# Loading v as bf16 through GpSimd's queue, with earlier first weights and the first q ahead of the token ids, in a fused attention and hash-routed expert kernel

## The chip, the cores and the metric

The kernel runs on one core of one Trainium2 chip. The metric is the device time in microseconds (us) of one execution, the median of several runs.

## The reference

Two steps, the second on the output of the first. `q`, `k`, `v` are f32 of shape (8 batches, 8 heads, 576 positions, 64).

```python
q_s = exp(q - max(q, axis=-1));  q_s /= sum(q_s, axis=-1)      # softmax over the 64 features
k_s = exp(k - max(k, axis=2));   k_s /= sum(k_s, axis=2)       # softmax over the 576 positions
kv  = einsum('bhsd,bhse->bhde', k_s, v)                         # 64 x 64 for each head
x   = einsum('bhsd,bhde->bhse', q_s, kv)                        # then (4608 tokens, 512)

expert = token_ids * 2654435761 % 8                             # so: the low three bits decide
for e in range(8):                                              # w1: 512 x 1024, w2: 1024 x 512
    out[expert == e] = relu(x[expert == e] @ w1[e]) @ w2[e]
```

The inputs are small (0.1 times a normal draw), and the kernel leaves the maxima out of both softmaxes.

## The kernel before, in words

**Order of the work.** The kernel keeps one instruction list for each engine (TensorE, VectorE, ScalarE, GpSimd, SP), filled by Python code in program order through `em.op` and `em.dma`. A small tracker (`Buf`, with the tokens of its last writers and readers) puts semaphore waits in front of an instruction where it reads or overwrites what another engine handles. Within an engine everything runs in list order, so the place of a call in the Python text is what sets the order of the work. There is no planner. A load is issued by the engine on whose list it stands: q, k, v and the token ids on SP, the expert weights and the stores on GpSimd. Loads that GpSimd issues may change the type on the way (the weights are f32 in memory and bf16 in SBUF).

**Routing.** The token ids (L288) become expert numbers, one-hot flags `flg` (L331), totals and prefix sums by two matmuls (L338, L339), and from them the position `pos` of each token within its group of 384 or 192 tokens, sorted by expert (L346 to L356). All that is VectorE's work and comes first in its list. `one_hot(b)` (L579) turns positions of batch b into a permutation matrix. `clear()` (L608) has GpSimd write zeros into the sorted activations `xT` once the flags are there. `segment_table()` and `widths()` (L359 to L414), behind batch 0, work out on VectorE and then on GpSimd where each expert's piece of each group goes.

**Stage one: the eight batches.** The loop over b (L734) does, for batch b, with buffers p = b % 2:

- `exp_k(p)` on ScalarE (L504), and `transpose_q(p)`: 18 transposes of exp(q) on TensorE into banks 0 to 2 (L514), copied out by VectorE (L524, L527) and ScalarE (L526);
- `sort(1 - p, ...)` twice: the batch before, times its permutation matrix (L588, 10 matmuls each, banks 3 to 5 and 0 to 2), copied to `xs` by ScalarE (L595); `fill` matmuls (L600) stand before and between, they compute nothing that is used;
- `cast_v(p)`: VectorE copies v from f32 `vf` to bf16 `vx` (L509). `vx` has 65 columns a head, the last of them one, so that the kv matmul sums exp(k) too;
- `load(b + 2, p)`: q, k and v of two batches on, 1,152 KB each, on SP (L495); each waits until its f32 buffer has been read;
- `one_hot(b + 1)` and `exp_q(1 - p, .)` for the next batch;
- `kv(p)`: 36 matmuls of 64 rows into banks 6 and 7, 130 columns each, two heads' v with their ones (L537); the two halves of the array take turns (`h2`). VectorE divides by the sums (L542, L546);
- `qsum(p)` (L556, L560): the sums of exp(q);
- GpSimd's `segments(b - 1)`: 16 copies (L638) of the sorted pieces from `xs` to their places in `xT`, behind 32 register loads (L621);
- `attend(p, ...)`: q times kv (L564), scaled by VectorE into `xn` (L569).

**Stage two: the experts.** For each expert, layer 1 (`l1`, L676, two halves of 320 columns at most) goes through PSUM into `hT` by a relu on ScalarE or VectorE (L683, L685), layer 2 (L701) into `yo` (L711, L713), and GpSimd scatters rows to the output (L717). The first units of layer 1 are mixed with the last batch (L790), and six more follow the last sort (L829), with PSUM banks 6, 3, 0, 6, 3, 0; after these `lslot()` hands out banks 0, 2, 4 in turn.

**Weights.** Four slots in SBUF, each for one w1 and one w2 in bf16, lie over buffers of stage one: slot 0 over qf0 and kf0, slot 1 over vf0 and qf1, slot 2 over kf1 and vf1, slot 3 over the exponentials. The first w1, in two halves (`weights1_half`, L661), is issued by GpSimd in the middle of `segments(5)` and waits for the last k (`R=[b_k[1]]`). The next weights (L653, L667) come in the last batch and after it.

Of the kernel before, what the change touches and what calls it, by code (L numbers as in the profile page):

```python
# [4 lines left out]
F32 = mybir.dt.float32  # L5
BF16 = mybir.dt.bfloat16
# [158 lines left out]
def fused_kernel(nc, q, k, v, moe_token_ids, moe_w1, moe_w2, out):  # L165
# [22 lines left out]
    def at(name, shape, dt, off=None):  # L188
        size = {F32: 4, BF16: 2, F16: 2, I32: 4, I64: 8}[dt]
        for n in shape[1:]:  # L190
            size *= n
        size = (size + 31) // 32 * 32
        if off is None:
            off = cur[0]
            cur[0] += size
        return nc.alloc_sbuf_tensor_at(name, shape, dt, offset=off)

    xT = at("xT", [128, 4, E * CAPS], BF16)
    qkv0 = cur[0]
    qf, kf, vf = [], [], []  # L200
    for i in range(2):
        qf.append(at("qf%d" % i, [128, 4, NC, DH], F32))
        kf.append(at("kf%d" % i, [128, 4, NC, DH], F32))
        vf.append(at("vf%d" % i, [128, 4, NC, DH], F32))
    exp0 = cur[0]
    eq = [at("eq%d" % i, [128, 2, NC, 2, DH], BF16) for i in range(2)]
    ek = [at("ek%d" % i, [128, 2, NC, 2, DH], BF16) for i in range(2)]
    vx0 = cur[0]
    vx = [at("vx%d" % i, [128, 4, NC, DH + 1], BF16) for i in range(2)]
    qT = [at("qT%d" % i, [128, 2, 2, T * 128], BF16) for i in range(2)]  # L210
# [7 lines left out]
    hT = [at("hT%d" % i, [128, FC, CAP], BF16) for i in range(2)]  # L218
    selA = at("selA", [128, B * T, 128], BF16, vx0)
    selB = at("selB", [128, NG * TG, 2, B * T], BF16, vx0 + 10240)  # L220

    w1b, w2b, wreg = [], [], [qkv0, qkv0 + 18432, qkv0 + 36864, exp0]
    for i, o in enumerate(wreg):
# [51 lines left out]
    def gp(fn, R=(), W=(), P=()):  # L275
        em.op("pool", fn, R, W, P)
# [4 lines left out]
    def ac(fn, R=(), W=(), P=()):  # L281
# [4 lines left out]
                             "thr")}  # L286
    b_tok = Buf()
    em.dma("sync", "d_tok", lambda e: e.dma_start(  # L288
        tok64[:], moe_token_ids.rearrange("(b p c) -> p b c", b=B, p=64, c=NC)), P=[b_tok])
    b_vx = [Buf(), Buf()]  # L290
    b_qT = [[Buf() for _ in range(3)] for _ in range(2)]
# [15 lines left out]
    for i in range(2):  # L307
        gp(lambda e, i=i: e.memset(vx[i][:, :, :, DH:DH + 1], 1.0), P=[b_vx[i]])
        gp(lambda e, i=i: e.memset(qT[i][:, :, :, S:T * 128], 1.0), P=b_qT[i])
        for g in range(2):  # L310
            gp(lambda e, i=i, g=g: e.memset(xs[i][:, :, XO[g] + GW[g]:XO[g] + GW[g] + SEG[g]], 0.0), P=b_xs[i])
        for h in range(2):
            dv(lambda e, i=i, h=h: e.memset(kvn[i][64 * h:64 * h + 64, :, 1 - h, :], 0.0), P=[b_kvn[i]])
# [169 lines left out]

    b_q, b_k, b_v = [Buf(), Buf()], [Buf(), Buf()], [Buf(), Buf()]
    b_eq = [[Buf(), Buf()] for _ in range(2)]
# [7 lines left out]
    def load(b, p):  # L493
        for nm, dst, src, bb in (("d_q%d", qf, q, b_q), ("d_k%d", kf, k, b_k), ("d_v%d", vf, v, b_v)):
            em.dma("sync", nm % p, lambda e, dst=dst, src=src: e.dma_start(  # L495
                dst[p][:].rearrange("p h c d -> p h (c d)"),
                src[b].rearrange("(a h) (p c) d -> (h p) a (c d)", h=2, p=64)), W=[bb[p]])

# [4 lines left out]
    def exp_k(p):  # L503
        ac(lambda e: e.activation(ek[p][:].rearrange("p j c a d -> p a (j c) d"),  # L504
                                  kf[p][:].rearrange("p (a j) c d -> p a (j c) d", a=2), ACTF.Exp),
           R=[b_k[p]], W=[b_ek[p]])

    def cast_v(p):
        dv(lambda e: e.tensor_copy(out=vx[p][:, :, :, 0:DH], in_=vf[p][:]), R=[b_v[p]], W=[b_vx[p]])  # L509

# [19 lines left out]

    def kv(p):
        fns = []
        for j in range(2):
            for c in range(NC):
                for h2 in range(2):
                    r = slice(64 * h2, 64 * h2 + 64)
                    fns.append(lambda e, j=j, c=c, h2=h2, r=r: e.matmul(  # L537
                        PB[:, 6 + h2, 130 * j:130 * j + 130], ek[p][r, j, c, :, :].rearrange("p a d -> p (a d)"),
                        vx[p][r, j::2, c, :], start=(c == 0), stop=(c == NC - 1)))
        em.op("pe", fns, R=[b_ek[p], b_vx[p]], W=[bk[6], bk[7]])  # L540
        KV = PB[:, 6:8, 0:260].rearrange("p h (j a x) -> p j h a x", j=2, a=2)
        dv(lambda e: e.reciprocal(out=rk[p][:].rearrange("p (j h) -> p j h", h=2), in_=KV[:, :, :, 0, 64]),  # L542
           R=[bk[6], bk[7]], W=[b_rk[p]])
        for a in range(2):
            r = slice(64 * a, 64 * a + 64)
            dv(lambda e, a=a, r=r: e.tensor_tensor(  # L546
                out=kvn[p][r, :, a, :].rearrange("p (j h) x -> p j h x", h=2), in0=KV[r, :, :, a, 0:DH],
                in1=rk[p][r, :].rearrange("p (j h) -> p j h", h=2).unsqueeze(3).to_broadcast([64, 2, 2, DH]),
                op=ALU.mult), R=[bk[6], bk[7], b_rk[p]], W=([b_kvn[p]] if a == 0 else ()),
               P=(() if a == 0 else [b_kvn[p]]))  # L550
# [176 lines left out]

    load(0, 0)
    load(1, 1)
    clear()  # L730
    one_hot(0)
    exp_q(0, 0)
    exp_q(0, 1)
    for b in range(B):  # L734
# [4 lines left out]
        if b > 0:  # L739
# [5 lines left out]
            sort(1 - p, 2, 0)  # L745
        cast_v(p)
        if b + 2 < B:
            load(b + 2, p)
        if not last:
            one_hot(b + 1)  # L750
            exp_q(1 - p, 0)
            exp_q(1 - p, 1)
        kv(p)
        qsum(p)
        if b == B - 2:
            for s, bs in enumerate(([b_q[0], b_k[0]], [b_v[0], b_q[1]])):
                b_w1[s], b_w2[s] = [Buf(*bs), Buf(*bs)], Buf(*bs)
            load_segments(b - 1, "pool")
            sg = segments(b - 1)
            run(sg, 8)  # L760
            weights1_half(0, 0, 0, R=[b_k[1]])
            weights1_half(0, 0, 1)
            run(sg)
        elif last:
            weights1(1, 1)
            weights2(0, 0)
            for x in (b - 1, b):
                load_segments(x, "pool", 1)
                load_segments(x, "dve", 0)
            run(segments(b - 1, "pool", 1))  # L770
        elif b > 0:
            load_segments(b - 1, "pool")
            run(segments(b - 1))
# [12 lines left out]

    for s, bs in ((2, [b_k[1], b_v[1]]), (3, b_eq[0] + b_eq[1] + b_ek)):
        b_w1[s], b_w2[s] = [Buf(*bs), Buf(*bs)], Buf(*bs)
# [40 lines left out]
    for i, (ee, f) in enumerate([(0, f) for f in range(FC // 2, FC, 2)] + [(1, f) for f in range(0, FC, 2)]):  # L829
        l1(ee, f, 0, (6, 3, 0)[i % 3], True)  # L830
    for f in range(0, FC, 2):
# [38 lines left out]
    fresh = lambda: Buf(every)  # L870
    for lst in (b_q, b_k, b_v, b_ek, b_vx, b_kvn, b_rk, b_rq, bk):
        lst[:] = [fresh() for _ in lst]
# [24 lines left out]
    b_xg, b_id, b_yg = [fresh() for _ in range(4)], fresh(), [fresh() for _ in range(T)]  # L897
    dv(lambda e: e.memset(vx[0][:, :, :, DH:DH + 1], 1.0), P=[b_vx[0]], R=[every])
    dv(lambda e: e.memset(qT[0][:, :, :, S:T * 128], 1.0), P=b_qT[0])
# [6 lines left out]
    for b in range(B):  # L906
        load(b, 0)
        exp_q(0, 0)
        exp_q(0, 1)
        exp_k(0)  # L910
        cast_v(0)
        transpose_q(0)
        kv(0)
        qsum(0)
# [67 lines left out]
```

## Time and profile before

| | us |
|---|---|
| median of 3 runs | 228.6 (228.36 to 228.71) |
| the profiled execution, its time | 228.91 |
| its span, first to last instruction | 227.1 |
| TensorE busy, matmuls | 199.1 (88% of the span) |
| TensorE, weight loads | 130.9 (58%) |
| VectorE | 123.8 (55%) |
| GpSimd | 118.0 (52%) |
| ScalarE | 106.6 (47%) |

The core read 61.90 MB and wrote 10.49 MB of HBM. The median time from issue to landing was 15.3 us for q, 15.6 for k, 15.4 for v (eight each), 2.4 us for the token ids (36 KB), and 5.6 us for each of the four pieces of the first w1.

The profile names lines of the kernel (L537 is line 537) and engines: PE is TensorE, PEld its weight loads, DVE VectorE, ACT ScalarE, POOL GpSimd, SP the engine that issues plain loads. A timeline line gives the start, the busy time, the engine, the line, the operation, what is written <- what is read, the number of instructions, and in brackets how long the engine had stood idle and who released it. The forty digits are tenths of busy time in slices of 5.7 us. In the GB/s row a casting load counts by the bytes written.

### The profile page before, as it was taken

How to read it: one execution, taken by the hardware profiler on the slowest of the kernel's cores; microseconds unless marked ns; L12 is line 12 of the kernel's file. 1: busy time of each engine (PE TensorE's matmuls, PEld its weight loads, DVE VectorE, ACT ScalarE, POOL GpSimd, SP SyncE). 2: the span in 40 equal slices, each digit the busy share in tenths (PEclk: the TensorE clock that was granted, in tenths of full speed). 3: DMA queues.
4: the chain of work that ended last, by engine and by line, in shares of the span. 5: the costliest groups of instructions: out<-in, count | busy, mean ns of one | idle time of the engine just before them, and what ended most of it. 6: DMA issues, size and time to landing. Idle time of an engine off the chain costs nothing.

```text
span 227.1 us, 4693 instructions
## 1 busy us (share of the span) xinstructions
PE 199.1 (88%) x1804; PEld 130.9 (58%) x1828; DVE 123.8 (55%) x273; ACT 106.6 (47%) x133; POOL 118.0 (52%) x227
## 2 busy tenths in 40 slices
PE   0538868999989789899999999999999999999990
PEld 0336546767667566674664854754845845846640
DVE  5778999888988845999912412411422412412220
ACT  3548687797888826654541331332322322422311
POOL 6500859894584993940007975706616525035053
PEclk9999999999999999999999999999999999999996
DMA  5999999999999999999964899999999798113032
GB/s 144 403 391 393 390 389 391 391 392 389 389 390 389 243 170 195 160 184 205 211 113 185 155 193 205 365 244 209 273 203 279 123 208 238 42 46 149 16 123 101
DMA packets 29775, 54.96 MB, mean 242 GB/s; under 512 B 2351, under 2 KB 11567, under 8 KB 29744
## 3 DMA queue, kind: packets, MB, share of 16 engines
q0 software_dynamic: 16544, 26.22, 55.0%
q1 hardware_dynamic: 13200, 28.35, 33.9%
q8 instruction: 16, 0.26, 0.5%
q14 instruction: 15, 0.12, 0.2%
HBM read 61.90 MB, written 10.49 MB: 319 GB/s over the span
## 4 chain that ended last, share of the span: by engine, by line
PE 63%; DVE 12%; DMA 12%; issue 4%; POOL 3%; ACT 2%; SPq 2%; POOLq 1%; DVEq 0%; ACTq 0%
PE ps L701 29%; PE ps L676 24%; DMA kf<-in_k_dram 7%; DMA vf<-in_v_dram 5%; DVE xn L569 4%; PE ps L588 4%; PE ps L537 2%; SPq L495 2%; POOL xT L638 2%; PE ps L564 1%; DVE vx L509 1%; DVE kvn L546 1%; ACT eq L500 1%; PE ps L600 1%; DVE zz L436 1%
## 5 line engine op out<-in xcount | busy, mean ns | idle before, releaser
L717 POOL DMA_INDIRECT out_dram<-yo,idx x40 | 39.5, 988 | 72.6 <-ACT yo L711 31.9
L701 PE MATMUL ps<-w2b,hT 128*128 128x512 bf16 x312 | 68.6, 379 | 0.4
L676 PE MATMUL ps<-xT,w1b 128*128 128x320 bf16 (+1 forms) x512 | 64.6, 286 | 1.7 <-DVE cs L438 0.9
L676 PEld LDWEIGHTS ps<-xT,w1b 128*128 128x128 bf16 x512 | 49.7, 98 | 16.1 <-DVE cs L438 1.2
L701 PEld LDWEIGHTS ps<-w2b,hT 128*128 128x128 bf16 x320 | 31.2, 98 | 36.3
L638 POOL COPY xT<-xs x112 | 42.1, 433 | 16.6 <-ACT xs L595 14.2
L683 ACT ACTIVATE hT<-ps 128x640 bf16<-128x640 f32 x41 | 28.8, 703 | 40.0 <-PE ps L676 39.6
L711 ACT ACTIVATE yo<-ps 128x512 f32<-128x512 f32 x26 | 15.5, 597 | 54.1 <-PE ps L701 54.1
L685 DVE TENSOR_SCALAR hT<-ps 128x640 bf16<-128x640 f32 x23 | 19.0, 824 | 30.2 <-PE ps L676 30.2
L713 DVE COPY yo<-ps 128x512 f32<-128x512 f32 x14 | 9.7, 691 | 44.0 <-PE ps L701 44.0
L588 PE MATMUL ps<-oneh,xn 128*128 128x384 bf16 (+1 forms) x160 | 23.4, 295 | 3.3 <-DVE xn L569 2.8
L569 DVE TENSOR_TENSOR xn<-ps,rq 128x1024 bf16<-128x1024 f32 (+1 forms) x24 | 23.6, 1039 | 4.2 <-PE ps L564 4.2
L588 PEld LDWEIGHTS ps<-oneh,xn 128*128 128x128 bf16 x160 | 14.4, 97 | 14.4 <-DVE xn L569 5.7
L595 ACT ACTIVATE xs<-ps 128x768 bf16<-128x768 f32 (+1 forms) x32 | 19.0, 647 | 7.0 <-PE ps L588 6.8
L500 ACT ACTIVATE eq<-qf 128x1152 bf16<-128x1152 f32 x16 | 17.7, 1159 | 8.5 <-DMA qf<-in_q_dram 8.5
L504 ACT ACTIVATE ek<-kf 128x2304 bf16<-128x2304 f32 x8 | 17.0, 2124 | 4.9 <-DMA kf<-in_k_dram 4.8
L537 PE MATMUL ps<-vx,ek 64*128 64x130 bf16 x288 | 10.6, 228 | 4.0 <-DVE vx L509 4.0
L514 PE MATMUL ps<-ident,eq 128*128 128x128 bf16 x144 | 10.5, 231 | 2.8 <-ACT eq L500 1.9
L667 POOL DMA_DIRECT2D w2b<-in_moe_w_dram x16 | 12.4, 803 | 0.0
L537 PEld LDWEIGHTS ps<-vx,ek 64*128 64x128 bf16 x288 | 9.2, 99 | 5.4 <-issue 5.2
L564 PEld LDWEIGHTS ps<-kvn,qT 128*128 128x128 bf16 x160 | 9.3, 99 | 5.2 <-DVE kvn L546 5.1
L600 PE MATMUL ps<-ones,ident 128*128 128x512 bf16 x26 | 9.2, 390 | 3.3 <-DVE qT L527 2.3
(102 smaller groups left out, 146.8 us busy)
## 6 DMA issues: line engine op xcount, KB each, us to landing
qf<-in_q_dram SPq DMA_DIRECT2D x8, 1152.0 KB, 15.3
kf<-in_k_dram SPq DMA_DIRECT2D x8, 1152.0 KB, 15.6
vf<-in_v_dram SPq DMA_DIRECT2D x8, 1152.0 KB, 15.4
w2b<-in_moe_w_dram POOLq DMA_DIRECT2D x16, 512.0 KB, 12.2
w1b<-in_moe_w_dram POOLq DMA_DIRECT2D x14, 512.0 KB, 10.3
w1b<-in_moe_w_dram POOLq DMA_DIRECT2D x4, 256.0 KB, 5.6
out_dram<-yo,idx POOLq DMA_INDIRECT x40, 4.1
tok<-in_moe_token_ids_dram SPq DMA_DIRECT2D x1, 36.0 KB, 2.4
```

What stands on the lines that cost most here:

```text
L500: ac(lambda e: e.activation(eq[p][:, j, :, :, :].rearrange("p c a d -> p a c d"), qf[p][:, j::2, :, :], ACTF.Exp), R=[b_q[p]], W=[b_eq[p][j]])
L504: ac(lambda e: e.activation(ek[p][:].rearrange("p j c a d -> p a (j c) d"), kf[p][:].rearrange("p (a j) c d -> p a (j c) d", a=2), ACTF.Ex ...
L537: fns.append(lambda e, j=j, c=c, h2=h2, r=r: e.matmul(PB[:, 6 + h2, 130 * j:130 * j + 130], ek[p][r, j, c, :, :].rearrange("p a d -> p (a ...
L569: dv(lambda e: e.tensor_tensor(out=xn[p][:, t0:t0 + n, :].rearrange("p t (g x) -> p (t g) x", x=DH), in0=PB[:, bank:bank + n, :].rearrange ...
L588: em.op("pe", [lambda e, g=g, i=i, k=k, n=n: e.matmul(PB[:, bank + (k if g == 0 else 2), (0 if g == 0 else GW[1] * k):(GW[0] if g == 0 els ...
L595: ac(lambda e, g=g, src=src: e.activation(xs[p][:, c0:c0 + 2, XO[g]:XO[g] + GW[g]], src, ACTF.Copy), R=bs, P=b_xs[p][c0:c0 + 2])
L638: return e.tensor_copy(out=xT[:, :, bass.ds(do, SEG[g])], in_=xs[p][:, :, XO[g]:XO[g] + GW[g] + SEG[g]][:, :, bass.ds(so, SEG[g])])
L676: em.op("pe", [lambda e, d=d, k=k: e.matmul(cut(PB[:, u + k, 0:H2]), w1b[s][:, d, 128 * (f + k):128 * (f + k) + 128], cut(rhs(d)), start=( ...
L683: ac(lambda e: e.activation(o, i, ACTF.Relu), R=bk[u:u + 2], W=[b_hT[hp][hf][f // 2]])
L685: dv(lambda e: e.tensor_scalar(out=o, in0=i, scalar1=0.0, scalar2=None, op0=ALU.max), R=bk[u:u + 2], W=[b_hT[hp][hf][f // 2]])
L701: em.op("pe", [lambda e, fc=fc: e.matmul(PB[:, u, :], hT[hp][:, fc, 128 * t:128 * t + 128], w2b[s][:, fc, :], start=(fc == 0), stop=(fc == ...
L717: em.dma("pool", "d_o%d" % y, lambda e: e.indirect_dma_start(out=out[:, :], out_offset=IndirectOffsetOnAxis(ap=idx[:, 5 * ee + t:5 * ee + ...
```

## The change

- v is no longer loaded as f32 by SP and cast by VectorE. A new `load_v` on GpSimd's list loads it straight into bf16, into one of four buffers: `vx` is now two tensors, each `[128, 5, 2, 9, 64]`, with a block of ones in the middle (index 2) and one v on either side of it (indices 0, 1 and 3, 4).
- v of batch b + 1 is issued in batch b, ahead of `segments(b - 1)` on GpSimd; the first two right at the start, ahead of `clear()`, the first of them waiting for the first q.
- `kv` reads three blocks of 64 columns (two heads and the ones), so its matmuls have 192 columns in place of 130.
- The first q is issued ahead of the token ids on SP. `one_hot(0)` moves from ahead of the loop to behind the first transposes.
- Without vf, slot 1 lies over qf1 and kf1, slot 2 over the exponentials, slot 3 over vx. The first w1 is issued right behind the last v and ahead of all of `segments(5)`; it no longer waits for the last k.
- The six units of layer 1 use banks 6, 3, 0, 6, 4, 2.

The same lines change in the branch for overflowing experts, which this input does not enter. The diff without that branch:

```diff
-    vx = [at("vx%d" % i, [128, 4, NC, DH + 1], BF16) for i in range(2)]
+    vx = [at("vx%d" % i, [128, 5, 2, NC, DH], BF16) for i in range(2)]
...
-    w1b, w2b, wreg = [], [], [qkv0, qkv0 + 18432, qkv0 + 36864, exp0]
+    w1b, w2b, wreg = [], [], [qkv0, qkv0 + 18432, exp0, vx0]
...
+    def load_one(nm, dst, src, b, p, bb):
+        em.dma("sync", nm % p, lambda e: e.dma_start(
+            dst[p][:].rearrange("p h c d -> p h (c d)"),
+            src[b].rearrange("(a h) (p c) d -> (h p) a (c d)", h=2, p=64)), W=[bb[p]])
+
+    load_one("d_q%d", qf, q, 0, 0, b_q)
     em.dma("sync", "d_tok", lambda e: e.dma_start(
         tok64[:], moe_token_ids.rearrange("(b p c) -> p b c", b=B, p=64, c=NC)), P=[b_tok])
-    b_vx = [Buf(), Buf()]
+    b_vx = [Buf() for _ in range(4)]
...
-        gp(lambda e, i=i: e.memset(vx[i][:, :, :, DH:DH + 1], 1.0), P=[b_vx[i]])
+        gp(lambda e, i=i: e.memset(vx[i][:, 2, :, :, :], 1.0), P=b_vx[2 * i:2 * i + 2])
...
+        load_one("d_q%d", qf, q, b, p, b_q)
+        load_one("d_k%d", kf, k, b, p, b_k)
+
+    def load_v(b, n, R=()):
+        o = 3 * (n % 2)
+        em.dma("pool", "d_v%d" % n, lambda e: e.dma_start(
+            vx[n // 2][:, o:o + 2, :, :, :].rearrange("p a j c d -> p (a j) (c d)"),
+            v[b].rearrange("(a h) (p c) d -> (h p) a (c d)", h=2, p=64)), R=R, W=[b_vx[n]])
...
-    def cast_v(p):
-        dv(lambda e: e.tensor_copy(out=vx[p][:, :, :, 0:DH], in_=vf[p][:]), R=[b_v[p]], W=[b_vx[p]])
...
-    def kv(p):
+    def kv(p, n):
+        o, one = (0, 2) if n % 2 == 0 else (2, 0)
+        a0 = 1 - one // 2
...
-                        PB[:, 6 + h2, 130 * j:130 * j + 130], ek[p][r, j, c, :, :].rearrange("p a d -> p (a d)"),
-                        vx[p][r, j::2, c, :], start=(c == 0), stop=(c == NC - 1)))
+                        PB[:, 6 + h2, 192 * j:192 * j + 192], ek[p][r, j, c, :, :].rearrange("p a d -> p (a d)"),
+                        vx[n // 2][r, o:o + 3, j, c, :], start=(c == 0), stop=(c == NC - 1)))
...
-    load(0, 0)
+    load_one("d_k%d", kf, k, 0, 0, b_k)
     load(1, 1)
+    load_v(0, 0, R=[b_q[0]])
+    load_v(1, 1)
     clear()
-    one_hot(0)
     exp_q(0, 0)
     exp_q(0, 1)
...
-        cast_v(p)
+        if b == 0:
+            one_hot(0)
...
-        kv(p)
+        kv(p, b % 4)
         qsum(p)
+        if 0 < b < B - 1:
+            load_v(b + 1, (b + 1) % 4)
         if b == B - 2:
-            for s, bs in enumerate(([b_q[0], b_k[0]], [b_v[0], b_q[1]])):
+            for s, bs in enumerate(([b_q[0], b_k[0]], [b_q[1], b_k[1]])):
                 b_w1[s], b_w2[s] = [Buf(*bs), Buf(*bs)], Buf(*bs)
+            weights1_half(0, 0, 0)
+            weights1_half(0, 0, 1)
             load_segments(b - 1, "pool")
-            sg = segments(b - 1)
-            run(sg, 8)
-            weights1_half(0, 0, 0, R=[b_k[1]])
-            weights1_half(0, 0, 1)
-            run(sg)
+            run(segments(b - 1))
...
-    for s, bs in ((2, [b_k[1], b_v[1]]), (3, b_eq[0] + b_eq[1] + b_ek)):
+    for s, bs in ((2, b_eq[0] + b_eq[1] + b_ek), (3, b_vx)):
...
-        l1(ee, f, 0, (6, 3, 0)[i % 3], True)
+        l1(ee, f, 0, (6, 3, 0, 6, 4, 2)[i], True)
```

## The prediction

> **What bounds the kernel now.** I read the page's forty slices first, then the chain of waits, then the timelines of TensorE, VectorE and GpSimd one by one.
>
> ```profile
> PE   0538868999989789899999999999999999999990
> DMA  5999999999999999999964899999999798113032
> GB/s 144 403 391 393 390 389 391 391 392 389 389 390 389 243 170 195 160 184 205 211 113 185 155 193 205 365 244 209 273 203 279 123 208 238 42 46 149 16 123 101
> ```
>
> The loads run at 390 GB/s up to about 75 us, so stage one (attention and routing of the eight batches) looks bound by them. From 97 us TensorE is full to the end (99.5% busy in each stretch of 10 us from 100 to 220) and nothing there waits for a weight. So the end moves with the time at which stage one hands over. What paces stage one has to be read from one turn of its loop:
>
> ```profile
> 58.78 1.48 PE L588 MATMUL ps<-oneh,xn 128*128 128x384 bf16 x10 [0.34 <-DVE xn L569]
> 60.32 0.38 PE L600 MATMUL ps<-ones,ident 128*128 128x512 bf16 x1
> 60.54 1.47 PE L588 MATMUL ps<-oneh,xn 128*128 128x384 bf16 x10
> 61.94 1.21 PE L537 MATMUL ps<-vx,ek 64*128 64x130 bf16 x36
> 63.08 0.65 PE L556 MATMUL ps<-pair,qT 128*128 128x2 bf16 x20
> 64.34 1.29 PE L564 MATMUL ps<-kvn,qT 128*128 128x128 bf16 x20 [0.15 <-DVE kvn L546]
> 67.41 1.48 PE L588 MATMUL ps<-oneh,xn 128*128 128x384 bf16 x10 [0.34 <-DVE xn L569]
> ```
>
> ```profile
> 60.04 1.35 DVE L509 CAST vx<-vf 128x2304 bf16<-128x2304 f32 x1
> 61.71 1.14 DVE L579 TENSOR_SCALAR oneh<-col,pos 128x384 bf16<-128x384 f16 x5 [0.32 <-PE ps L588]
> 63.19 0.18 DVE L542 RECIPROCAL rk<-ps 128x4 f32<-128x4 f32 x1 [0.34 <-PE ps L537]
> 63.41 0.87 DVE L546 TENSOR_TENSOR kvn<-ps,rk 64x256 bf16<-64x256 f32 x2
> 65.00 2.95 DVE L569 TENSOR_TENSOR xn<-ps,rq 128x1024 bf16<-128x1024 f32 x3 [0.28 <-PE ps L564]
> ```
>
> A loop that bites its tail: sort (L588), fill, sort, kv (L537), then VectorE's kvn, attend (L564), two pieces of xn, and sort again. 58.78 to 67.41 is 8.63 us. The kv groups start at 25.51, 35.53, 44.69, 53.31, 61.94, 70.56 and 79.47, so three turns of 8.62. The loads need 9.0 us a batch (landings of k at 56.90, 65.88, 74.89); they had a lead and catch up only at the last k (kv at 79.47, 0.29 late). The cast at 60.04 ends at 61.39, and VectorE then waits for TensorE twice: it lies beside the loop. kv lies on it.
>
> ```profile
> 28.86 0.19 POOL L414 CAST widei<-wide 128x8 int32<-128x8 f32 x1
> 31.33 13.43 POOL L638 COPY xT<-xs  x32 [2.28 <-issue]
> 45.91 5.50 POOL L638 COPY xT<-xs  x16 [1.15 <-ACT xs L595]
> 54.53 5.49 POOL L638 COPY xT<-xs  x16 [3.12 <-ACT xs L595]
> ```
>
> GpSimd has a backlog from 23 to 45 us (routing tables until 29.05, 2.3 us of register loads, 32 segment copies), then room.
>
> **What the Trainium skill says.** "DMA: Bandwidth & Descriptors", section "SWDGE vs HWDGE vs iDMA": a casting load must come from GpSimd, and each DMA engine takes turns between GpSimd's and SP's queues. So a v load beside q and k loads gets about half the rate; no trace line of before shows the two kinds contending for long (casting w1 meets the last v only at 75 to 78 us), so this is unproven here. "SBUF — State Buffer", section "Who interferes with whom": VectorE's two-port operations block GpSimd. The trace fits (L638 copies took 0.42 us each at 31 to 45 us, 0.34 later), and a v load's descriptors could suffer so too. "TensorE: Matmul & The Clock Gate", section "Wait — 56ns, not 53.3ns?": time goes by columns, at half speed when cold. It agrees: 8 matmuls of 320 columns in L676 start 1.09 us apart per group, 0.426 ns a column; the first kv, after idle time, took 2.13 us against 1.21.
>
> **The change, part by part.**
>
> *Cast removed, 8 x 1.36 us of VectorE.* Covered in turns 3 to 6, as shown. In turns 1 and 2 sort ends as late as the cast (kv at 25.51, the cast ends 25.26), so no gain there. In the last turn the cast ran 77.78 to 79.14 and the second sort ended at 79.5: a tie. Gain 0; bounds 0 to -0.3.
>
> *kv wider.* The ones become a third block of 64 columns: 192 instead of 2 x 65 = 130. Two halves of the array run as a pair. Now 36 matmuls take 1.15 us start to start of the next group (61.94 to 63.08), 64 ns a pair. 192 columns at 0.426 ns are 82 ns: 18 x 82 = 1.47 us, +0.33 a batch. All of it is on the loop, for kv(1) to kv(7): 7 x 0.33 = **+2.3**. Bounds: 2.2, as 82 does not fit into 64, to 3.8, if the 1.15 scales by 192/130. A gain is excluded.
>
> *Start.* q0 issues at 0.80 instead of 1.60 and lands near 5.9 instead of 7.3. The token ids now queue behind q0: landing near 6.8 instead of 3.2. VectorE needed 7.8 us from them to the positions (3.27 to 11.01), so positions at 13.5 to 14.6. In VectorE's order the q transposes' copies (0.96) and one_hot(0) and (1) (2.27) follow: free at 16.8 to 17.8. The old order had VectorE take up 1/kv sums at 17.04. v0 waits on GpSimd for q0, is issued near 6.2 and shares with k0 and q1: data from 7.3 to 13.3, landing 14.4, close to the old cast's end (14.72). But the cold kv(0) grows from 2.13 to about 3.0 us: 17.4. So the sums come 0.4 to 0.8 later. k1, after six loads rather than five, lands near 22 instead of 19.39; its exp (2.12) and the ScalarE copy (1.00) end at 25.1, then the second sort 1.4, kv(1) near 26.5. Between these I take **+0.8** at kv(1); bounds 0 to 1.5. The memsets of the ones grow from 36 to 1152 columns; the nearest row (960 f32 columns, 0.85 us) says under 1.6 us in all: GpSimd is free at 6.1 instead of 4.5, covered by the wait for q0. clear() waits for flags later, with GpSimd idle until 23 anyway.
>
> *v loads queued on GpSimd.* Each issue costs about 0.8 us there (L667, as many rows: 0.803). v2 stands behind the routing tables, whose end was 29.05 and moves to about 29.7. A casting load of about that size takes from 7.6 us (L667's least for 1.05 MB of source) to 9 at half rate (an estimate, from the first page's turn-taking), with q4 and k4 queued on SP: v2 lands at 36 to 39, say 37.9. kv(2) would be ready at 26.3 + 10.02 + 0.33 = 36.65. **+1.3** for the wait; bounds 0 to 2.5. Behind it on GpSimd the copies start later: 2.3 + 16 copies = 8 us, v3 issued near 39.5, landing 47.5, just when kv(3) is ready (37.9 + 9.16 + 0.33 = 47.4). After that a turn of GpSimd is 0.8 + 2.3 + 5.5 = 8.6 us against a turn of the loop of 8.95, and v is issued 11 us ahead: covered. If copies stay at 0.42 us the turn is 9.8 and the cover is gone, 0.85 a turn.
>
> *q and k alone on SP* run ahead, so the last k is no longer waited for: **-0.3**.
>
> *Weights.* w1(0) is issued behind v7, before the segment copies of batch 5, instead of between them. By then k7 has landed, by the above, so no one waits; were it not so, 2.1 MB of source, 5.3 us of loading, would share with k7, up to 2.6 us. First use of w1b was at 82.94, without a wait, so no gain either. Copies start 2.7 us later, GpSimd having had 3.1 us idle there. Region 1 now waits for exp of k7 (done by about 81), region 3 for kv(7): both before GpSimd gets to them. Cost 0, bounds -0.2 to +0.5.
>
> *Banks 6,3,0,6,4,2.* TensorE stood from 95.90 to 96.77; VectorE's cs is named, but that matmul needs bank 0, which ScalarE emptied at 96.62. The new order frees it: **-0.9**; 0 if something else was late.
>
> Sum: 2.3 + 0.8 + 1.3 - 0.3 - 0.9 = +3.2 us. The profiled execution took 228.91 (span 227.1 and 1.8 around it): 232.1. It lies 0.3 above the median, so 231.8 against 228.6.
>
> **Rivals.** *Faster, 226.9:* the loads or VectorE pace the loop after all. For it: 390 GB/s without a gap, VectorE 86 to 95% busy. Then 0.8 us of earlier loads brings k7 to 74.1 and kv(7), 4.6 us behind it, to 78.7; the wider kv hides in TensorE's waits, and with the banks 228.9 - 0.8 - 0.9 = 227.2, median 226.9. Against it: turns of 8.62, shorter than the loads' 9.0. It decides if kv costs under 0.1 us a turn and v2 is in time. *v late every turn, 235:* copies at 0.42 us or descriptors blocked, 4 turns x 0.85 = 3.4 on top: 235.2. Against: 0.34 us copies from 45 us on. *No difference, 228.6:* v2 in time, no loss at the start, kv at half its price.
>
> **How the numbers follow.** Forecast 0.60, its own range 229.6 (all low ends) to 234.5 (all high ends together would be 236); faster rival 0.20; late v 0.12; no difference 0.08. A measurement of this kernel tells 0.2% from no change. The range 227.0 to 235.0 leaves out half of the faster rival, half of the late v and a little of the forecast. Faster 0.20, same 0.08, slower 0.72.
>
> **What would show it.** kv groups of 64x192 taking 1.5 us and turns near 8.95; kv(2) waiting for DMA of v at about 38; kv(1) near 26.3; kv(7) near 83; no stop of TensorE ahead of L676's last third. I am wrong if kv groups still take 1.2 us, or kv(7) starts before 80.

## The result, and the profile after

The changed kernel takes 233.93 us (median of four runs, 233.78 to 234.02) against 228.66 for the kernel before on the same chip: the ratio is 1.0229, with a 95% interval of 1.0211 to 1.0247. It is slower, as forecast, but by 5.3 us where the forecast said 3.2. The profiled execution took 234.02, its span 232.3 (before: 228.91 and 227.1).

The page of the kernel after: the slices of TensorE and of the loads, the kv group, and how long a v load takes from issue to landing.

```profile
PE   0408796899998987999999999999999999999990
...
DMA  6999999999997999769993699999999799213023
GB/s 210 367 292 305 397 290 314 311 377 301 297 370 161 144 185 202 120 84 199 205 212 105 172 189 206 269 327 203 292 196 244 169 187 241 83 45 140 21 104 117
...
L547 PE MATMUL ps<-vx,ek 64*128 64x192 bf16 x288 | 14.7, 258 | 6.5 <-DMA vx<-in_v_dram 6.5
...
vx<-in_v_dram POOLq DMA_DIRECT2D x8, 576.0 KB, 9.6
```

Three things are to be seen. The GB/s row is below before's even 390 in most slices up to 69 us: a casting load counts by the bytes written, half of those read, so that 290 to 315 means both kinds at once and not idle DMA engines (the DMA row stays at 9 there). The kv group has 64x192 where it had 64x130. And its one large wait in the whole run, 6.5 us, is for a DMA of v. In which turn that is, the chain of waits tells at its head:

```profile
0.79 6.06 DMA qf<-in_q_dram
7.16 10.95 DMA vx<-in_v_dram
18.20 3.08 PE ps L547 x36
```

The very first kv waits: v0 is issued at 7.16, soon after q0 has landed, and lands 10.95 us later. TensorE's timeline of the kernel before has this group 3.33 us earlier, behind the cast:

```profile
14.87 2.13 PE L537 MATMUL ps<-vx,ek 64*128 64x130 bf16 x36 [4.01 <-DVE vx L509]
```

Here is a turn of the loop later on, TensorE's timeline of the kernel after (kv is L547 now, sort L598, attend L574):

```profile
64.52 1.48 PE L598 MATMUL ps<-oneh,xn 128*128 128x384 bf16 x10 [0.34 <-DVE xn L579]
66.06 0.38 PE L610 MATMUL ps<-ones,ident 128*128 128x512 bf16 x1
66.28 1.47 PE L598 MATMUL ps<-oneh,xn 128*128 128x384 bf16 x10
67.67 1.66 PE L547 MATMUL ps<-vx,ek 64*128 64x192 bf16 x36
69.27 0.65 PE L566 MATMUL ps<-pair,qT 128*128 128x2 bf16 x20
70.52 1.29 PE L574 MATMUL ps<-kvn,qT 128*128 128x128 bf16 x20 [0.15 <-DVE kvn L556]
73.59 1.48 PE L598 MATMUL ps<-oneh,xn 128*128 128x384 bf16 x10 [0.34 <-DVE xn L579]
```

It is the old turn with the same two small waits and nothing new but a longer kv: 64.52 to 73.59 is 9.07 us instead of 8.63, and from the start of kv to the next group 1.60 instead of 1.14.

The starts of the kv groups say where the time came from (us):

| | kv(0) | kv(1) | kv(2) | kv(3) | kv(6) | kv(7) | span |
|---|---|---|---|---|---|---|---|
| before | 14.87 | 25.51 | 35.53 | 44.69 | 70.56 | 79.47 | 227.1 |
| after | 18.20 | 29.47 | 39.95 | 49.53 | 76.75 | 85.38 | 232.3 |
| difference | 3.33 | 3.96 | 4.42 | 4.84 | 6.19 | 5.91 | 5.2 |

Of the 5.2 us, 3.96 are there at kv(1). From kv(1) to kv(6) five turns add 2.23, 0.45 each, the width of kv; the last turn gives back 0.28 although its kv is wider too. Behind kv(7) come a last 0.45 of kv, -1.04 where the banks changed (below), and -0.1 that I can't assign.

### The profile page after: what moved, and what is told of

Its sections match the earlier page's. It is cut to its first block, busy times and chain, and to the rows that moved or that the text cites. A ratio compares the mean times of both kernels' runs of the same rounds, so it can differ in the third digit from the quotient of the medians.

```text
span 232.3 us, 4687 instructions
## 1 busy us (share of the span) xinstructions
PE 202.2 (87%) x1804; PEld 134.6 (58%) x1828; DVE 112.8 (49%) x265; ACT 106.7 (46%) x133; POOL 121.1 (52%) x235
## 4 chain that ended last, share of the span: by engine, by line
PE 74%; DVE 13%; DMA 7%; issue 3%; DVEq 1%; POOL 1%; POOLq 0%
PE ps L711 29%; PE ps L686 26%; PE ps L598 8%; DVE xn L579 7%; PE ps L547 6%; DMA vx<-in_v_dram 5%; DVE kvn L556 3%; DMA qf<-in_q_dram 3%; PE ps L574 2%; PE ps L610 1%; DVEq L634 1%; POOL out_dram L727 1%; DVE rk L552 1%; PE ps L823 1%; DVE qT L532 1%
## 5 line engine op out<-in xcount | busy, mean ns | idle before, releaser
L686 PE MATMUL ps<-xT,w1b 128*128 128x320 bf16 (+1 forms) x512 | 64.4, 286 | 0.8 <-ACT hT L693 0.8
L686 PEld LDWEIGHTS ps<-xT,w1b 128*128 128x128 bf16 x512 | 49.8, 98 | 14.9 <-ACT hT L693 1.1
L648 POOL COPY xT<-xs x112 | 39.1, 407 | 19.4 <-ACT xs L605 17.9
L598 PE MATMUL ps<-oneh,xn 128*128 128x384 bf16 (+1 forms) x160 | 23.2, 294 | 2.8 <-DVE xn L579 2.8
L598 PEld LDWEIGHTS ps<-oneh,xn 128*128 128x128 bf16 x160 | 14.5, 98 | 13.6 <-DVE xn L579 5.7
L547 PE MATMUL ps<-vx,ek 64*128 64x192 bf16 x288 | 14.7, 258 | 6.5 <-DMA vx<-in_v_dram 6.5
L547 PEld LDWEIGHTS ps<-vx,ek 64*128 64x128 bf16 x288 | 12.8, 100 | 7.8 <-issue 7.7
L589 DVE TENSOR_SCALAR oneh<-col,pos 128x384 bf16<-128x384 f16 (+1 forms) x40 | 9.9, 317 | 9.8 <-PE ps L598 9.8
L574 PEld LDWEIGHTS ps<-kvn,qT 128*128 128x128 bf16 x160 | 9.0, 98 | 5.1 <-DVE kvn L556 5.1
```

The source lines that it names most:

```text
L547: fns.append(lambda e, j=j, c=c, h2=h2, r=r: e.matmul(PB[:, 6 + h2, 192 * j:192 * j + 192], ek[p][r, j, c, :, :].rearrange("p a d -> p (a ...
L598: em.op("pe", [lambda e, g=g, i=i, k=k, n=n: e.matmul(PB[:, bank + (k if g == 0 else 2), (0 if g == 0 else GW[1] * k):(GW[0] if g == 0 els ...
L648: return e.tensor_copy(out=xT[:, :, bass.ds(do, SEG[g])], in_=xs[p][:, :, XO[g]:XO[g] + GW[g] + SEG[g]][:, :, bass.ds(so, SEG[g])])
L686: em.op("pe", [lambda e, d=d, k=k: e.matmul(cut(PB[:, u + k, 0:H2]), w1b[s][:, d, 128 * (f + k):128 * (f + k) + 128], cut(rhs(d)), start=( ...
```

## The experiments

All times are medians; ratios are to the kernel before on the same chip, with a 95% interval. Line numbers shift by a few lines between the kernels. The theories after the result: *the loop of TensorE and VectorE paces stage one from kv(1) on, and the order in which the loads' bytes come paces it before that.* The rivals: the token ids, now behind q0, hold the start (VectorE's routing chain); v loads come late in every turn; the loads pace the loop, so kv's width counts for little.

### kv with 128 columns

```diff
-        o, one = (0, 2) if n % 2 == 0 else (2, 0)
-        a0 = 1 - one // 2
+        o = 3 * (n % 2)
...
-                        PB[:, 6 + h2, 192 * j:192 * j + 192], ek[p][r, j, c, :, :].rearrange("p a d -> p (a d)"),
-                        vx[n // 2][r, o:o + 3, j, c, :], start=(c == 0), stop=(c == NC - 1)))
+                        PB[:, 6 + h2, 128 * j:128 * j + 128], ek[p][r, j, c, :, :].rearrange("p a d -> p (a d)"),
+                        vx[n // 2][r, o:o + 2, j, c, :], start=(c == 0), stop=(c == NC - 1)))
```

> The changed kernel with 128 columns in each kv matmul: the block of ones is not read, so the sums of exp(k) are left out and the division uses a column of v instead. If the wider kv lies on the loop (theory), kv groups take about 1.15 us again, the turn falls from 9.07 to 8.62 us, the cold first kv from 3.06 to 2.1, and the time by 7 x 0.45 + 0.95 = 4.1 us, to about 229.8. If the loads or another engine pace the loop (rival), the turn stays near 9.0 and the time falls by less than 1.3 us.

Measured: 230.93, ratio 1.0094 (1.0063 to 1.0126), so 3.1 us of the 5.3 gone. TensorE's timeline of this kernel:

```profile
39.70 1.18 PE L546 MATMUL ps<-vx,ek 64*128 64x128 bf16 x36 [0.55 <-DMA vx<-in_v_dram]
48.79 1.18 PE L546 MATMUL ps<-vx,ek 64*128 64x128 bf16 x36
57.38 1.18 PE L546 MATMUL ps<-vx,ek 64*128 64x128 bf16 x36
65.97 1.18 PE L546 MATMUL ps<-vx,ek 64*128 64x128 bf16 x36
```

The turns are 8.59 again (57.38 to 65.97): the whole step from 8.6 to 9.07 is kv's columns, and a loop paced by loads would not have moved. The gain is 1.0 us less than expected. About half of that is lost by kv(1): the cold first kv takes 0.95 us less (2.11), but attend behind it takes 2.34 us instead of 1.29, and kv(1) comes only 0.47 earlier, at 29.00. The first of the lines above has the other half: kv(2) could start a little earlier than in the kernel after, and now waits 0.55 us for v2. The kernel after reaches kv(2) at 39.95, where a weight load waits 0.2 us for v2 and no matmul does: the load is the next ceiling, just above.

### Cast taken out of the kernel before

Two runs. In the first, nothing is cast and v is left out of the result:

```diff
-        cast_v(p)
...
-        gp(lambda e, i=i: e.memset(vx[i][:, :, :, DH:DH + 1], 1.0), P=[b_vx[i]])
+        gp(lambda e, i=i: e.memset(vx[i][:], 1.0), P=[b_vx[i]])
```

> The kernel before without VectorE's cast of v: v is loaded as before, but kv reads constants, so v is left out of the result. If the cast lay beside the loop (prediction), turns 3 to 6 stay at 8.62 us and only the start gains, where the first kv no longer waits for v0 and its cast (14.87 before, about 13.6 then): the time falls by 0.5 to 1.5 us, to about 227.6. If VectorE paced the loop (rival), each turn falls by up to 1.36 us until the loads stop it at 9.0 a batch or TensorE does, and the time falls by 2 us or more.

Measured: 229.0, ratio 1.001 (0.9998 to 1.0022). The turns are as before (kv at 63.08 and 71.70), but the memsets of the whole `vx`, 2.04 us each on GpSimd, disturbed the start of this kernel (last section), so its total decides nothing. In the second, the first two batches are cast as ever and the others not:

```diff
-        cast_v(p)
+        if b < 2:
+            cast_v(p)
```

> The kernel before with VectorE's cast of v for batches 0 and 1 only; the later batches use the v of these (the products with v are wrong from batch 2 on), so that the start is undisturbed. If the cast lies beside the loop (theory), turns 3 to 6 stay at 8.62 us and the time falls by 0 to 0.3 us. If VectorE paces the loop (rival), the time falls by 1 us or more, as far as the loads, 9.0 us a batch, let it.

Measured: 228.81, ratio 0.9994 (0.9985 to 1.0004). VectorE's timeline, and then TensorE's, of this kernel:

```profile
62.07 1.14 DVE L579 TENSOR_SCALAR oneh<-col,pos 128x384 bf16<-128x384 f16 x5 [1.59 <-PE ps L588]
```

```profile
62.29 1.21 PE L537 MATMUL ps<-vx,ek 64*128 64x130 bf16 x36
70.92 1.21 PE L537 MATMUL ps<-vx,ek 64*128 64x130 bf16 x36
```

Where VectorE did the cast it now stands idle for 1.59 us and waits for TensorE's sort; the turn is 8.63. The cast lay beside the loop, and taking eight of them from VectorE (its busy time fell from 123.8 to 112.8 us in the kernel after) bought nothing.

### v0 ahead of everything on GpSimd

```diff
+    em.dma("pool", "d_v0", lambda e: e.dma_start(
+        vx[0][:, 0:2, :, :, :].rearrange("p a j c d -> p (a j) (c d)"),
+        v[0].rearrange("(a h) (p c) d -> (h p) a (c d)", h=2, p=64)), W=[b_vx[0]])
     b_qT = [[Buf() for _ in range(3)] for _ in range(2)]
...
-    load_v(0, 0, R=[b_q[0]])
```

> The changed kernel with v of batch 0 issued as the first entry of GpSimd's list, without waiting for the first q. If v0 was late because its bytes stood behind those of q1 and k1 (theory), kv(0) starts near 14.5 instead of 18.20 and the time falls by 3.0 to 3.7 us, to about 230.6. If the token ids behind q0 set the start (rival: VectorE is busy with them and with the permutations until 17.06), the division still starts near 20 or later, and the time falls by at most 1.3 us. A third case: q0 and k0 are delayed by v0 by as much as is won, and the time is unchanged.

Measured: 234.33, ratio 1.0238 (1.0206 to 1.0271): a miss, no gain at all. TensorE's timeline, then GpSimd's:

```profile
14.55 3.06 PE L550 MATMUL ps<-vx,ek 64*128 64x192 bf16 x36 [1.50 <-DVE prod L362]
...
26.90 1.66 PE L550 MATMUL ps<-vx,ek 64*128 64x192 bf16 x36
...
40.01 2.94 PE L550 MATMUL ps<-vx,ek 64*128 64x192 bf16 x36 [2.54 <-DMA vx<-in_v_dram]
```

```profile
29.26 0.88 POOL L509 DMA_DIRECT2D vx<-in_v_dram  x1
```

kv(0) starts at 14.55 with the token ids still behind q0, and the division at 18.33, not near 20. In the kernel after, then, the ids do not hold the start: VectorE is through with them at 17.06 and stands idle for 4.25 us before the division. They are next in line, though. Here v0 also shares with the ids, VectorE gets them at 8.84 instead of 7.21, and it goes from its last permutation to the division without a pause. kv(1) comes 2.6 us earlier than in the kernel after, and there the gain ends: kv(2) waits 2.54 us for v2, which GpSimd issues at 29.26 and whose bytes appear only after 32 us (the rate falls from 394 to 275 GB/s from 32 on), when k3 is nearly in; and after the pause kv(2) itself takes 2.94 us instead of 1.66. So the late v0 had hidden the wait for v2 that I had predicted.

### q1 and k1 held back until k0 has landed

```diff
+    em.raw("sync", lambda e: None, R=[b_k[0]])
     load(1, 1)
     load_v(0, 0, R=[b_q[0]])
```

> The changed kernel with SP waiting for the landing of k0 before it issues q1 and k1; v0 is still issued at about 7.2 us. If v0 was late because of bytes queued ahead of it (theory), its bytes now follow k0 at once, it lands near 12.5 and the DMA rate has no gap between 9 and 11 us; kv(0) then starts 4 to 5 us earlier, but q1 and k1 come 2 to 4 us later, and the time falls by 1 to 3 us. If a casting load from GpSimd takes 3.7 us from its issue to its first byte whatever is in the queue (rival), the DMA rate falls to near zero between about 9 and 11 us and v0 lands near 15.

Measured: 234.37, ratio 1.0241 (1.0206 to 1.0275). The total is a miss, but the start answers the question of why v0 is late. Here are stretches of one microsecond of the kernel after (start and end, length, busy time and number of instructions of TensorE, its weight loads, VectorE, ScalarE and GpSimd; the last three columns are the granted clock, the DMA engines' busy share and GB/s):

```profile
10.00:11.00 1.00, 1.00 (x13) 1.00 (x11) 0.97 (x2) 0.98 (x1) 1.00 (x2) 1.00 1.07 396
11.00:12.00 1.00, 0.71 (x7) 0.44 (x5) 0.94 (x2) 1.00 (x1) 1.00 (x2) 1.00 1.08 349
12.00:13.00 1.00, 0.00 (x0) 0.00 (x0) 0.96 (x2) 1.00 (x2) 0.38 (x1) 1.00 1.12 282
13.00:14.00 1.00, 0.00 (x0) 0.00 (x0) 0.86 (x3) 0.27 (x2) 0.00 (x0) 1.00 1.14 293
```

And of this kernel, with q1 and k1 held back:

```profile
8.00:9.00 1.00, 0.07 (x1) 0.07 (x2) 0.81 (x3) 1.00 (x2) 0.95 (x3) 1.00 1.04 374
9.00:10.00 1.00, 1.00 (x7) 0.66 (x8) 0.21 (x1) 0.15 (x2) 1.00 (x2) 1.00 0.96 108
10.00:11.00 1.00, 1.00 (x12) 1.00 (x11) 0.97 (x2) 1.00 (x1) 1.00 (x2) 1.00 1.09 182
11.00:12.00 1.00, 0.67 (x7) 0.41 (x4) 0.93 (x3) 1.00 (x2) 1.00 (x2) 1.00 1.20 192
```

In the kernel after, the rate stays at 390 to 396 GB/s until 11 us, which is what plain loads do alone; only then does it fall to 282 to 296, where a casting load shares with a plain one. v0 was issued at 7.16, so its bytes began more than four microseconds later. SP had issued q0, k0, q1 and k1 by 4.1 us. Here SP holds q1 and k1 back until 9.89. v0 is issued at the same time, 7.12, and the rate drops to 108 to 192 GB/s as soon as k0 is in: the bytes are v0's own, and kv(0) starts at 13.75. That refutes the rival of 3.7 us from the issue whatever is queued.

The packets in the traces carry the queue they came from, and they set a limit to the theory. In the kernel after, the first packet of v0 moves at 11.55 us, behind the rest of k0 and four fifths of q1; the last of q1 and all of k1, issued before it, share with it. In this run it moves at 8.95, with the last packets of k0. In all runs that load v in this way, wherever a v was issued behind the first 7 us with GpSimd's queue empty, the first packet came 1.4 to 1.8 us later if SP had at most 0.6 of a load issued and not yet moved, 3.0 to 3.2 us later if it had 1.1 to 1.2 loads, and 3.8 to 4.4 us later, never more, if it had 1.4 to 2.7. So in these runs such a load waits for what SP has issued, but for one and a half loads of 1,152 KB at the most.

kv(1) still comes 2.29 us earlier than in the kernel after, at 27.18. All of it is lost on the way to kv(2), at 40.50: a stall of VectorE at 34 us takes 1.4 us and a slow sort behind it 1.3 (both in the last section). Without them little would have been left either, since v2's last packet moves at 39.09.

### Every v a batch earlier

v0 first as above, and v of batch b + 2 issued in batch b:

```diff
-        if 0 < b < B - 1:
-            load_v(b + 1, (b + 1) % 4)
+        if b < B - 2:
+            load_v(b + 2, (b + 2) % 4)
```

> The changed kernel with v0 as GpSimd's first entry, as in the run that issued it first, and every later v issued one batch earlier, so that v2 stands ahead of the routing tables on GpSimd. Theory now: two ceilings lie side by side at kv(2). The late v0 holds it at 39.95 us, and v2, landing near 39.8, holds it at 40 when v0 is early; so only both together gain. Then kv(1) starts near 26.9, kv(2) near 37.4, no matmul waits for a load of v, and the time falls by 2.5 us against the changed kernel, to about 231.4. Rival: the early loads of v hold up q1 and k1, kv(1) comes 2 us later than 26.9 and the time falls by less than 1 us.

Measured: 235.68, ratio 1.0309 (1.0282 to 1.0335), the worst of all: the rival of this run came true. ScalarE's timeline, then TensorE's:

```profile
25.24 2.12 ACT L518 ACTIVATE ek<-kf 128x2304 bf16<-128x2304 f32 x1 [4.58 <-DMA kf<-in_k_dram]
```

```profile
28.33 2.74 PE L601 MATMUL ps<-oneh,xn 128*128 128x384 bf16 x10 [3.14 <-ACT qT L537]
31.01 1.75 PE L550 MATMUL ps<-vx,ek 64*128 64x192 bf16 x36
```

v2, issued at 13.63, took its share of the rate while k1 was still coming: v2's packets move from 17.9 to 25.1 us, and k1's last at 23.3, against 20.5 with v0 alone moved ahead. exp of k1 begins at 25.24 (19.86 in the kernel after), ScalarE's copy of qT stands behind it, the sort behind that, and kv(1) starts at 31.01.

The same with kv of 128 columns, to see whether the width still counts in full when v is early:

```diff
+                        PB[:, 6 + h2, 128 * j:128 * j + 128], ek[p][r, j, c, :, :].rearrange("p a d -> p (a d)"),
+                        vx[n // 2][r, o:o + 2, j, c, :], start=(c == 0), stop=(c == NC - 1)))
...
+        if b < B - 2:
+            load_v(b + 2, (b + 2) % 4)
```

> The same with 128 columns in each kv matmul (the sums of exp(k) left out, the division by a column of v). If the change's loss consists of the start, the wait for v2 and the wider kv (theory), nothing of it is left but the gain of the banks: turns of 8.62 us, kv(7) near 79.8, and 227.3 us, 1.4 below the kernel before. If something else of the change costs time (rival), it stays above 228.7.

Measured: 231.95, ratio 1.0132 (1.0114 to 1.015). Against the run before it, on the same chip, that is 3.7 us (3.6 between the two profiled spans). From kv(2) to kv(7) it takes 43.04 us against 45.45: 2.41 less in five turns, so the width counts in full here too. Ahead of that it was 1.85 us ahead at kv(1) and lost 1.09 of it by kv(2), where VectorE stalled (last section). By the sign set for this run, the total above 228.7, something else costs time, and that is the order of the loads: I had taken early v as free, and kv(1) comes at 29.16.

### v2 behind k1

The kernel with every v a batch earlier, with kv of 192 columns and one wait more: v2 is issued when k1 has landed.

```diff
-            load_v(b + 2, (b + 2) % 4)
+            load_v(b + 2, (b + 2) % 4, R=[b_k[1]] if b == 0 else ())
```

> As the run that issued every v one batch earlier, but with the load of v2 waiting on GpSimd for the landing of k1. Theory now: until kv(2) the loads are the bound and only their order counts; v0 early held kv(2) by v2, v2 early held kv(1) by k1. With v2 right behind k1 the bytes come in the order in which they are needed: kv(1) starts near 26.9, kv(2) near 37.4, and the time is 2.5 us below the changed kernel, about 231.4; what is left against the kernel before is the wider kv. Rival: GpSimd's loads cost the start in any order (their descriptors, their ports, or the ids behind q0); then kv(2) starts at 39 or later again and the time stays above 233.4.

Measured: 231.43, ratio 1.0111 (1.0094 to 1.0128), as expected. GpSimd's timeline, then TensorE's:

```profile
21.76 0.74 POOL L509 DMA_DIRECT2D vx<-in_v_dram  x1 [8.22 <-DMA kf<-in_k_dram]
```

```profile
26.71 1.66 PE L550 MATMUL ps<-vx,ek 64*128 64x192 bf16 x36
...
37.59 1.66 PE L550 MATMUL ps<-vx,ek 64*128 64x192 bf16 x36
```

No matmul waits for v any more. kv(1) is 1.20 us later than before, kv(2) 2.06, and from there on each turn adds 0.45. With the bytes in the order of need, 2.5 us of the change's loss are gone, without a change of any amount of work: 233.93 to 231.43. That order is v0, then q1 and k1, then q2 and k2, with v2 joining in at 25.83 us, when three quarters of k2 are in. What is left against the kernel before: 1.20 at the start, about what the ids behind q0 cost alone (next run); 0.41 more in the turn to kv(2), of which 0.34 is one subtraction of VectorE that takes 0.50 us instead of 0.16 (last section); 3.15 of width; less 0.73, 1.04 and 0.1 for the last turn, the banks and the unassigned rest, 2.9 in all; the spans differ by 2.8.

### q0 ahead of the token ids, alone

The kernel before, with q0 ahead of the ids and `one_hot(0)` behind the first cast:

```diff
+    load_one("d_q%d", qf, q, 0, 0, b_q)
     em.dma("sync", "d_tok", lambda e: e.dma_start(
...
-    load(0, 0)
+    load_one("d_k%d", kf, k, 0, 0, b_k)
+    load_one("d_v%d", vf, v, 0, 0, b_v)
...
-    one_hot(0)
     exp_q(0, 0)
...
         cast_v(p)
+        if b == 0:
+            one_hot(0)
```

> The kernel before with only the first q issued ahead of the token ids, and the first permutation built behind the first cast. Here v0 still comes on SP. By the prediction's working the ids land near 6.8 instead of 3.2, VectorE's list is freed later than 17.04 and the division of batch 0 starts 0.4 to 0.8 us later: the time grows by 0.4 to 0.8 us, to about 229.2. By the rival the loads, started 0.8 us earlier, carry through to the end: the time falls by 0.5 to 0.8 us.

Measured: 229.02, ratio 1.001 (0.9999 to 1.002). kv(1) comes at 26.57, 1.06 later than before, about as I had priced it; at kv(7) it is 0.54 (80.01), since the last turn takes 8.37 us instead of 8.91: the later loop no longer waits for the last k. So of a microsecond lost at the start, half was slack. The interval of the total just includes no change, so the effect is read from the starts of the groups.

### The banks

The kernel after with the old banks, and, the other way round, the kernel before with the new ones:

```diff
-        l1(ee, f, 0, (6, 3, 0, 6, 4, 2)[i], True)
+        l1(ee, f, 0, (6, 3, 0)[i % 3], True)
```

> The changed kernel with the old order of PSUM banks, 6, 3, 0, 6, 3, 0. If that order caused the stop of TensorE of 0.88 us before the last third of the first layer-1 units (theory: the bank was still being emptied by ScalarE), the stop is back and the time is 0.9 us longer, 234.8. If VectorE's routing work caused it, as the releaser named in the trace says (rival), the time is unchanged within 0.2 us.

> The kernel before with only the order of the PSUM banks changed to 6, 3, 0, 6, 4, 2. Theory: the stop of 0.88 us goes and nothing else moves, so 228.66 - 0.9 = 227.8, a version that beats both. Rival: the stop was VectorE's, and the time stays within 0.2 us of 228.66.

Measured: 235.13, ratio 1.0284 (1.0254 to 1.0313), for the first, whose interval lies above that of the kernel after; 227.75, ratio 0.9965 (0.9949 to 0.9982), for the second. TensorE's timeline of the kernel after with the old banks, of the kernel after, and of the kernel before with the new ones:

```profile
95.66 6.68 PE L686 MATMUL ps<-xT,w1b 128*128 128x320 bf16 x48
103.23 6.05 PE L686 MATMUL ps<-xT,w1b 128*128 128x0 bf16 x48 [0.89 <-DVE cs L446]
```

```profile
95.56 12.58 PE L686 MATMUL ps<-xT,w1b 128*128 128x320 bf16 x96
```

```profile
89.63 12.58 PE L676 MATMUL ps<-xT,w1b 128*128 128x320 bf16 x96
```

The stop of 0.89 us comes and goes with the banks alone, while the `cs` that the profile names as its releaser is untouched. The name was wrong; the wait was for a bank still being emptied. In the old order the sixth unit writes bank 0, and the next one, the first that `lslot()` serves, takes bank 0 again. ScalarE's and TensorE's timelines of the kernel before show it:

```profile
95.92 0.70 ACT L683 ACTIVATE hT<-ps 128x640 bf16<-128x640 f32 x1 [0.38 <-PE ps L676]
96.77 6.05 PE L676 MATMUL ps<-xT,w1b 128*128 128x0 bf16 x48 [0.88 <-DVE cs L438]
```

From the first of these matmuls to the first of layer 2 it is 13.67 us before and 12.63 after, 1.04 less (13.46 and 12.41 in the two crossed kernels). The kernel before with this edit is the fastest of all that were run, 0.35% (some 0.8 us) ahead of before, and so beats both kernels.

### The first weights at their old place

```diff
-            weights1_half(0, 0, 0)
-            weights1_half(0, 0, 1)
             load_segments(b - 1, "pool")
-            run(segments(b - 1))
+            sg = segments(b - 1)
+            run(sg, 8)
+            weights1_half(0, 0, 0, R=[b_k[1]])
+            weights1_half(0, 0, 1)
+            run(sg)
```

> The changed kernel with the first w1 issued as before, in the middle of the segment copies of batch 5 and behind the landing of k7. Prediction: the place of the first weights costs and gains nothing, since no matmul waited for them: within 0.3 us of 233.93. Rival: the early weights share the loads with k7 and v7 and cost up to 2.6 us; then this kernel is faster by that.

Measured: 234.58, ratio 1.0257 (1.0234 to 1.0279). That is 0.65 above the kernel after, more than the 0.3 expected, but the intervals overlap. The kv groups start within 0.4 us of after's, already from kv(0) on (18.43), where the edit has no hand, and L686 waits for no weight in either. The place of the weights is worth nothing that these runs resolve.

## Why the prediction was right on the side and short on the size

| term of the sum | predicted | measured | by |
|---|---|---|---|
| start, at kv(1) | +0.8 (0 to 1.5) | +3.96 | 29.47 against 25.51 |
| kv wider, kv(1) to kv(7) | +2.3 (2.2 to 3.8) | +3.15 | 7 x 0.45 |
| wait for v2 at kv(2) | +1.3 (0 to 2.5) | 0 | kv(2) at 39.95; only a weight load waits, 0.2 |
| last k | -0.3 | -0.73 | last turn 8.63 against 8.91 with 0.45 more of kv |
| banks | -0.9 | -1.04 | the stop of 0.88 that has gone, and 0.16 around it |
| cast, weights | 0 | 0 | two casts only; weights at the old place |
| not assigned | | -0.1 | |
| sum | +3.2 | +5.2 | of the span |

**The step that failed** is the start's "data from 7.3 to 13.3, landing 14.4" for v0. v0 was issued at 7.16 (I had said 6.2; q0 landed at 6.85, not 5.9). The failure is the next clause: I let its bytes flow at once, sharing with k0 and q1. They came from 11.55 us, after one and a half loads that SP had issued before, then at half the rate, and landed at 18.1. Holding q1 and k1 back gave back the v0 that I had priced (kv(0) at 13.75). I had cited "DMA: Bandwidth & Descriptors" of the Trainium skill for turn-taking between the two queues; its section "Queues, rings and completion order" says again that each engine goes round the queues that have work, a packet at a time. The runs agree with that once both flow (about 43 packets of each queue in half a microsecond; 282 to 296 GB/s written, where one casting load and one plain at equal bytes read would write three quarters of 390, 293); they don't agree with a share from the moment of issue. What makes a queue wait for its first turn, and why for four microseconds at the most, I have not separated.

All the other steps of the start were near: the cold kv(0) took 3.06 us (about 3.0 said), VectorE was free at 17.06 (16.8 to 17.8), and with the order mended, v0 first and v2 behind k1, kv(1) comes 1.20 us later than before, within the bounds.

**kv's width** was the right mechanism at the wrong size. I had priced 192 columns at 0.426 ns, 82 ns a pair, and let the old pair of 64 ns stand for 130 columns without asking what in it was not columns. The three widths measured are 62, 64 and 88 ns (18 pairs in 1.11, 1.14 to 1.15 and 1.59 to 1.60 us, for 128, 130 and 192): 0.42 ns a column and a fixed 8 to 9 ns a pair. "TensorE: Matmul & The Clock Gate", section "Wait — 56ns, not 53.3ns?", gives columns at 2.4 GHz and 2.5 ns for a matmul; the slope agrees, the fixed part of these pairs on two halves of the array is larger. 0.45 against 0.33, seven times, is 0.8 us of the 2.0 that the sum fell short.

**The wait for v2** was real but hidden: issue at 31.84 (29.7 said), and kv(2) itself came 2 to 3 us later than I had it, because of v0. It showed when kv(2) could start earlier: 0.55 us with 128 columns, 2.54 with v0 first. Two items that I had added were alternatives: the start and this wait have the same loads behind them, and the later of the two is paid. That the total still fell inside the stated 227.0 to 235.0 owes something to luck: the start was 3.2 us dearer than priced, and the 1.3 us of this wait, not paid, took part of that back.

**The last k**: I read its wait as 0.29 us, the last turn (8.91) against the others (8.62). A last turn that waits for nothing is shorter than the others, 8.16 (82.73 less 74.57) in the run with 128 columns, so it had cost more, and more came back.

**The rivals.** That the loads or VectorE pace the loop is refuted by the run with 128 columns and by the one with two casts. v late in every turn did not come: turns are 9.07 from kv(3) on, and no matmul of kv but the first waits for v. Its ground, GpSimd's copies of 0.42 us, had gone with the cast (last section): the first 16 copies of the kernel after take 5.53 us, 0.35 each. That it makes no difference fell with the width and the start.

## What to carry to other kernels

In these runs a load that moved to a second queue did not get its share from the moment of issue: count what the other queue has already issued and put it ahead, up to the one and a half loads (4.4 us) that were seen here. When loads come at full rate without a gap, making one earlier makes another later, so list them in the order of need and check the next need down the list before counting a gain (here v0, then v2, then k1 each became the last). And time saved on an engine that waits for another one in each turn was worth nothing, while 62 columns more on the one it waits for counted in full, turn after turn.

## What the runs showed of the hardware that I had not expected

*VectorE held up by GpSimd.* In the kernel that holds q1 and k1 back, VectorE's timeline has a 128x8 subtraction that takes ten times its usual time:

```profile
33.81 1.60 DVE L398 TENSOR_TENSOR zz<-gcum,gprv 128x8 f32<-128x8 f32 x1
35.33 0.16 DVE L400 TENSOR_TENSOR zz<-gprv 128x8 f32<-128x8 f32 x1
```

It has two inputs in SBUF and ends just when GpSimd's run of sixteen copies ends (29.85 to 35.38). "SBUF — State Buffer" of the Trainium skill, section "Who interferes with whom", says that such an operation contends with a GpSimd instruction that reads SBUF; the 1.60 us fits, and so do 1.82 for the same instruction in the run with early v and 128 columns and 0.50 in the one with v2 behind k1, but in the kernel after it took 0.16 beside the same copies, so it is no fixed price. A tensor_scalar of 64x40 integers took 4.85 us beside GpSimd's memsets, two of them long, in the kernel without casts; it took 1.26 in the kernel before and 0.18 in the kernel after, where no memset ran at that moment:

```profile
3.35 4.85 DVE L323 TENSOR_SCALAR e_i<-tok 64x40 int32<-64x40 int32 x1 [1.10 <-DMA tok<-in_moe_token_ids_dram]
```

*GpSimd held up by VectorE.* The prediction had laid the 0.42 us of GpSimd's copies in the kernel before to VectorE's two-port operations. With the cast left out from the third batch on, the same 32 copies take 11.17 us instead of 13.43, so the cast was the cause:

```profile
31.66 11.17 POOL L638 COPY xT<-xs  x32 [2.28 <-issue]
```

*The clock.* Behind the stalled subtraction of 1.60 us, TensorE had stood idle for 2.41 us. The stretches of that kernel show the clock granted next (the column behind the length and the five busy times is the clock):

```profile
34.00:36.00 2.00, 0.58 (x6) 0.28 (x4) 1.90 (x5) 1.19 (x2) 2.00 (x6) 1.00 1.12 273
36.00:38.00 2.00, 1.01 (x3) 0.42 (x4) 1.09 (x5) 0.00 (x0) 0.09 (x1) 0.76 1.12 301
38.00:40.00 2.00, 2.00 (x9) 1.03 (x7) 0.04 (x1) 0.04 (x1) 0.00 (x0) 0.50 1.07 372
```

The clock was 0.76 of full speed and then 0.50, and a sort of 1.47 us took 2.77. It fell likewise behind a pause of TensorE of 2.54 us (v0 first, 0.54) and one of 3.14 us (every v earlier, 0.50), but not behind one of 2.86 us (early v with 128 columns, 1.00), so the length of the pause alone does not decide it.
